# The last unit's output of a recurrent-attention and rational-MLP kernel: two copies on two engines, one transfer per chunk

## The chip, the cores and the metric

The kernel runs on one core of one Trainium2 chip. The metric is the device time of one execution in microseconds (us). A core has five engines with queues of their own: TensorE (PE in the profile; its weight loads are PEld), VectorE (DVE), ScalarE (ACT), GpSimd (POOL) and SyncE (SP, which here only issues transfers). Transfers between HBM and the on-chip memory are issued from the queues of SP, ACT and POOL and moved by 16 DMA engines.

## The reference

Inputs `q`, `k`, `v`, `f_logit` have the shape (4, 8, 768, 48): batch B, heads H, positions S, head size D.

```
f = 1.0 / (1.0 + np.exp(-f_logit))
for t in range(S):
    state = f[:, :, t, :, None] * state + np.einsum('bhd,bhe->bhde', k[:, :, t], v[:, :, t])
    y[:, :, t] = np.einsum('bhd,bhde->bhe', q[:, :, t], state)
x = y.transpose(0, 2, 1, 3).reshape(3072, 384)
h = x @ w_in                                   # 384 -> 2048
P = a[0] + a[1] * h + a[2] * h**2 + a[3] * h**3
Q = 1.0 + abs(b[0]) * abs(h) + abs(b[1]) * h**2
out = (P / (Q + 1e-06)) @ w_out                # 2048 -> 384, float32, (3072, 384)
```

## The kernel before, in words

The 3072 tokens are worked in 12 units, numbered 0 to 11, of 256 tokens each: unit n is block c = n // 4 of positions in batch b = n % 4. A unit has two chunks (j = 0, 1) of C = 128 tokens. The recurrence is done in its chunked form (cumulative sums of log gates on PE, scores, masks, states), and its output x goes through the MLP: `h` (PE, w_in), the rational function on DVE, ACT and by accumulating transfers of POOL, and `o` (PE, w_out).

Nothing is scheduled by a planner. `ORDER` is one written-out list of steps, and each engine's instruction stream is the steps in that order. A step is a name with its arguments: `o 11 1 12 16` is function `o` for unit 11, chunk 1, tiles 12 to 15 of the 16 tiles of 128 that make up 2048. Waits between engines are derived from the tiles that the steps read and write. A wait is on the tile as a whole: what reads a part of tile `op` waits for what was last written to that tile.

The end of the work, which the change concerns, is made of these steps for unit n:

- `gm n m0 m1` (line 444, DVE) finishes tiles m0 to m1 of `gall`, the values P/Q, with the reciprocals `qi` that `ex` (line 412, ACT) made.
- `o n j m0 m1` (line 452, PE) multiplies those tiles by w_out for chunk j and sums into the PSUM tile `op`, whose first index after the partition is the chunk.
- `oe n j0 j1 eng` (in `oe`, line 459) copies chunks j0 to j1 of `op` into the SBUF tile `osb` [128 partitions, 2 chunks, 384 float32]. With `s` ScalarE copies. `osb` has two buffers, so unit 11 takes the buffer that unit 9 used.
- `so n j0 j1 qu` (in `store`, line 467) stores them to HBM.

A chunk's 128 partitions hold its tokens as 2t + i: partition 64 i + t is token 2t + i. `store` therefore issues two transfers from SP: i = 0 for partitions 0 to 63, the even tokens of both chunks, and i = 1 for partitions 64 to 127, the odd tokens of both. Each has 64 partitions x 2 chunks = 128 rows of 384 float32 = 1536 bytes, 192 KB together. The view of the destination is, in (step, count) pairs, (768, 64), (49152, 2), (1, 384).

The last steps of the list, where unit 11's two chunks are accumulated alternately, are

```
o 11 1 8 12; o 11 1 12 16; so 10 0 2 s; o 11 0 12 16; oe 11 0 2 s; so 11 0 2 s
```

Of the kernel before, what the change touches and what calls it, by code (L numbers as in the profile page):

```python
# [28 lines left out]
def kernel(  # L29
# [431 lines left out]
    def store(n, j0, j1, qu="s"):  # L461
        s = unit(n)
        for i in range(2):
            dst = bass.AP(tensor=out.tensor,
                          offset=out.offset + (s["b"] * S + s["c"] * NT + j0 * C + i) * DM,
                          ap=[[2 * DM, R], [C * DM, j1 - j0], [1, DM]])
            (nc.scalar if qu == "a" else nc.sync).dma_start(out=dst, in_=s["osb"][R * i:R * i + R, j0:j1, :])
# [47 lines left out]
```

## Time and profile before

| what | value |
|---|---|
| time, median of 3 runs | 237.08 us (236.73 to 237.97) |
| the profiled execution's own time | 238.7 us |
| its span, first to last instruction | 237.0 us |
| busy in the span | PE 85%, DVE 87%, ACT 85%, POOL 33% |
| ACT copy `osb<-op`, 128x768 | 12 of them, 801 ns on average; the last 0.80 us at 231.46 |
| transfers `out_dram<-osb` | 24, from SP, 192 KB each, median 5.1 us from issue to landing; the last ones 2.7 and 2.8 us |

The span is that of the profiled execution alone; 1.7 us of its own time lie outside it. "Share" of the DMA is the mean busy share of 16 engines. A packet is one row of a transfer, or one small completion write.

### The profile page before, as it was taken

How to read it: one execution, taken by the hardware profiler on the slowest of the kernel's cores; microseconds unless marked ns; L12 is line 12 of the kernel's file. 1: busy time of each engine (PE TensorE's matmuls, PEld its weight loads, DVE VectorE, ACT ScalarE, POOL GpSimd, SP SyncE). 2: the span in 40 equal slices, each digit the busy share in tenths (PEclk: the TensorE clock that was granted, in tenths of full speed). 3: DMA queues.
4: the chain of work that ended last, by engine and by line, in shares of the span. 5: the costliest groups of instructions: out<-in, count | busy, mean ns of one | idle time of the engine just before them, and what ended most of it. 6: DMA issues, size and time to landing. Idle time of an engine off the chain costs nothing.

```text
span 237.0 us, 6907 instructions
## 1 busy us (share of the span) xinstructions
...
## 2 busy tenths in 40 slices
...
GB/s 134 248 223 206 197 204 254 206 215 118 154 260 203 255 240 111 88 117 239 245 255 195 171 232 259 190 251 157 169 198 174 183 88 188 204 170 186 133 142 133
DMA packets 62957, 45.00 MB, mean 190 GB/s; under 512 B 51408, under 2 KB 57296, under 8 KB 62928
## 3 DMA queue, kind: packets, MB, share of 16 engines
...
q14 instruction: 6, 0.05, 0.0%
q10 hardware_dynamic: 144, 0.00, 0.0%
...
## 4 chain that ended last, share of the span: by engine, by line
DVE 28%; ACT 25%; PE 21%; DMA 14%; issue 7%; SPq 3%; ACTq 0%
DMA z<-h 8%; PE hp L345 8%; ACT hy L359 7%; PE op L452 7%; ACT qi L412 6%; DMA kn<-in_k_dram 5%; DVE h L363 5%; DVE gall L431 4%; SPq L110 3%; DVE scm L254 3%; ACT lq L404 3%; DVE gall L444 3%; DVE qkp L212 3%; DVE z L371 3%; PE y L268 2%
## 5 line engine op out<-in xcount | busy, mean ns | idle before, releaser
L452 PE MATMUL op<-w_out_sb,gall 128*128 128x384 bf16 x384 | 71.6, 330 | 2.8 <-DVE gall L444 2.0
L345 PE MATMUL hp<-xT,w_in_sb 128*128 128x256 bf16 x576 | 69.8, 279 | 2.3 <-ACT xT L324 2.2
L345 PEld LDWEIGHTS <-w_in_sb 128*128 128x128 bf16 x576 | 57.1, 100 | 13.2 <-issue 4.0
L359 ACT CAST hy<-hp 128x1024 bf16<-128x1024 f32 x48 | 47.8, 1028 | 7.3 <-PE hp L345 7.1
L452 PEld LDWEIGHTS <-gall 128*128 128x128 bf16 x384 | 35.4, 98 | 27.0 <-DVE gall L444 4.4
L404 ACT ACTIVATE lq<-z 128x2048 f32<-128x2048 bf16 (+1 forms) x25 | 45.5, 1826 | 1.9 <-DMA z<-h 1.8
L412 ACT ACTIVATE qi<-lq 128x2048 bf16<-128x2048 f32 (+1 forms) x26 | 46.4, 1799 | 0.1
L435 POOL DMA_DIRECT2D gall<-hy x21 | 20.2, 992 | 74.2 <-ACT lq L404 18.4
L399 POOL DMA_DIRECT2D z<-h x20 | 18.8, 954 | 49.7 <-DVE z L371 12.6
L363 DVE TENSOR_TENSOR h<-hy 128x2048 bf16<-128x2048 bf16 (+1 forms) x26 | 29.5, 1137 | 4.4 <-ACT hy L359 4.3
L254 DVE TENSOR_TENSOR scm<-sc,mask 128x1024 bf16<-128x1024 f32 x24 | 28.9, 1216 | 2.2 <-PE sc L246 2.2
L444 DVE TENSOR_TENSOR gall<-gall,qi 128x2048 bf16<-128x2048 bf16 (+1 forms) x26 | 29.5, 1139 | 1.0 <-ACT qi L412 1.0
L431 DVE TENSOR_TENSOR gall<-gall,h 128x2048 bf16<-128x2048 bf16 (+1 forms) x26 | 29.2, 1136 | 0.0
L261 POOL COPY vmp<-vn 128x128 bf16<-128x128 bf16 x24 | 25.2, 1126 | 9.7 <-DMA vn<-in_v_dram 9.6
L206 ACT ACTIVATE A<-cs 128x768 f32<-128x768 f32 (+1 forms) x26 | 19.4, 773 | 6.9 <-DVE qkp L212 6.2
L197 PE MATMUL cs<-lsp,Ui 128*128 128x384 bf16 (+1 forms) x39 | 12.1, 373 | 10.5 <-ACT lsp L187 10.1
L224 PE MATMUL tp<-ident,qkp 128*128 128x128 bf16 x192 | 14.6, 234 | 6.2 <-DVE scm L254 3.8
L212 DVE TENSOR_TENSOR qkp<-kn,A 128x768 bf16<-128x768 f32 (+1 forms) x13 | 11.7, 897 | 8.7 <-ACT A L206 4.6
L224 PEld LDWEIGHTS <-qkp 128*128 128x128 bf16 x192 | 12.4, 104 | 8.4 <-DVE qkp L212 6.2
L371 DVE TENSOR_SCALAR z<-hy 128x2048 uint16<-128x2048 uint16 (+1 forms) x26 | 16.7, 652 | 0.0
L182 ACT ACTIVATE fn<-fn 128x768 f32<-128x768 f32 (+1 forms) x13 | 10.6, 813 | 7.0 <-DMA fn<-in_f_logit_dram 7.0
L422 DVE TENSOR_SCALAR hy<-hy,a_sb 128x4096 bf16<-128x4096 bf16 (+1 forms) x13 | 16.4, 1259 | 0.0
...
## 6 DMA issues: line engine op xcount, KB each, us to landing
...
```

Source lines behind the costliest of these rows:

```text
L224: nc.tensor.transpose(t[:, x, i, p, :], s["qk"][:, x, i, 2 * p:2 * p + 2, :].rearrange("t h d -> t (h d)"), ident)
L254: return nc.vector.tensor_mul(t, s["sc", g].rearrange("s r a i t -> s (r a) (i t)"), mb)
L261: nc.gpsimd.tensor_copy(s["vm"][:, :, :, 32 * x:32 * x + 16], src)
L345: nc.tensor.matmul(t[:, m - m0, :].rearrange("f (j t) -> f j t", j=UB), w_in_sb[:, kk, m * P:(m + 1) * P], s["x"][:, :, kk, :], start=(kk ...
L359: nc.scalar.copy(fl(big(s, "hy", "hy", 3), m0, m1), fl(s["hp", m0], 0, m1 - m0))
L363: return nc.vector.tensor_mul(fl(big(s, "h2", "h2", 2), m0, m1), fl(s["hy"], m0, m1), fl(s["hy"], m0, m1))
L371: return nc.vector.tensor_scalar(fl(big(s, "z", "z", 2), m0, m1).bitcast(U16), fl(s["hy"], m0, m1).bitcast(U16), 0x7FFF, None, op0=ALU.bit ...
L404: nc.scalar.activation(fl(lq(s, g), m0 - 8 * g, m1 - 8 * g), fl(s["z"], m0, m1), AF.Ln, scale=regs[2], bias=1.0 + 1e-6)
L412: nc.scalar.activation(fl(s["qi", g], m0 - 8 * g, m1 - 8 * g), fl(s["lq", g], m0 - 8 * g, m1 - 8 * g), AF.Exp, scale=-1.0)
L431: return nc.vector.tensor_mul(fl(s["g"], m0, m1), fl(s["g"], m0, m1), fl(s["h2"], m0, m1))
L444: return nc.vector.tensor_mul(fl(s["g"], m0, m1), fl(s["g"], m0, m1), fl(s["qi", g], m0 - 8 * g, m1 - 8 * g))
L452: nc.tensor.matmul(s["op"][:, j, 0:DM], s["g"][:, m, C * j:C * j + C], w_out_sb[:, m, :], start=(s["on", j] == 1), stop=(s["on", j] == KF))
```

## The change

In the order list, the last four matmul tiles of chunk 0 come before those of chunk 1. Unit 11's copy is then split: chunk 0 by ScalarE, with a store from SP's queue, and chunk 1 by VectorE, with a store from ScalarE's queue. In `store`, a call for one chunk issues one transfer instead of two: its source is all 128 partitions of one chunk, and its destination view is (384, 2), (768, 64), (1, 384), with the parity i as the outermost of its three dimensions.

The other edits of the diff (an argument `hold` on the weight loads, a return value of `ls`, a record of every step's instruction in `marks`) are used by no step of the list and add no instruction.

```diff
-o 11 1 8 12; o 11 1 12 16; so 10 0 2 s; o 11 0 12 16; oe 11 0 2 s; so 11 0 2 s"""
+o 11 1 8 12; so 10 0 2 s; o 11 0 12 16; o 11 1 12 16; oe 11 0 1 s; so 11 0 1 s; oe 11 1 2 v; so 11 1 2 a"""
...
-    def load_w_in(m0, m1):
-        nc.gpsimd.dma_start(out=w_in_sb[:, :, m0 * P:m1 * P],
+    def load_w_in(m0, m1, hold=None):
+        i = nc.gpsimd.dma_start(out=w_in_sb[:, :, m0 * P:m1 * P],
...
+        if hold is not None:
+            behind(i, hold[1:])
...
     def store(n, j0, j1, qu="s"):
         s = unit(n)
+        if j1 - j0 == 1:
+            dst = bass.AP(tensor=out.tensor, offset=out.offset + (s["b"] * S + s["c"] * NT + j0 * C) * DM,
+                          ap=[[DM, 2], [2 * DM, R], [1, DM]])
+            (nc.scalar if qu == "a" else nc.sync).dma_start(out=dst, in_=s["osb"][:, j0, :])
+            return
         for i in range(2):
...
-            mark = args.pop()[1:] if args and args[-1].startswith("!") else None
-            made = steps[name](*(int(x.lstrip("@")) if x.lstrip("@").isdigit() else x for x in args))
-            if mark is not None:
-                marks[mark] = made
+            marks[".".join([name] + [x for x in args if x.isdigit()])] = steps[name](
+                *(int(x.lstrip("@")) if x.lstrip("@").isdigit() else x for x in args))
```

Here DM = 384, R = 64, C = 128.

More of the change, by code (lines that the diff above doesn't have):

```diff
@@ L19 @@
 ORDER = """
-cz 3; cz 0; cu 0; cz 1; ld 0 f 2 4; ci; ld 1 f; cu 1; ab_ b a; ld 0 k 0 2; ld 0 k 2 4; ld 0 v; ld 0 f 0 2; ld 0 q 0 2; ef 0 2 4; ls 0 2 4; fa; ef 0 0 2; ld 0 q 2 4; cz 2; cs 0 2 4 @2; ls 0 0 2; A 0 0 2 4; ld 1 q; cm; ld 2 f; ld 1 k; A 0 1 2 4; vm 0 1; cs 0 0 2 @1; xa 0 1 2 4; ld 1 v; ef 1; ls 1; xa 0 0 2 4; ab_ a s; wi 8 16; A 0 0 0 2; T 0 2 4 @0; vm 0 0; xa 0 0 0 2; A 0 1 0 2; xa 0 1 0 2; wi 4 8; cs 1 @2; Te 0 2 4; ef 2; ld 2 q; wi 0 4; ld 2 k; ld 3 f; T 0 0 2 @0; fr; vm 1 0; A 1 0; Te 0 0 2; sv 0 0 @3; sc 0 0 @1; sc 0 1 @0; A 1 1; ae 0; vm 1 1; st 0 0; ls 2; xa 1 1; cs 2 @2; mk 0 1; sv 0 1; xa 1 0; ld 2 v; wo 4 8; mk 0 0; A 2 1; T 1 @0; A 2 0; yi 0 1 @2; yb 0 2 4; wo 0 4; fb; yb 0 0 2; Te 1 s; st 0 1; sc 1 1 @3; ye 0 s; sc 1 0 @0; h 0 12 16 @1; mk 1 1; xa 2 0; hy 0 12 16; mk 1 0; ld 3 k; h 0 8 12 @2; hy 0 8 12; sq 0 8 16; ab 0 8 16; sv 1 0 @1; ld 3 q; h 0 4 8 @0; ae 1; hy 0 4 8; st 1 0; zv 0 8 16; h 0 0 4 @3; hy 0 0 4; ld 3 v; xa 2 1; yi 1 1 @0; ld 4 f; lz 0 8 16; sv 1 1; yb 1 2 4; yb 1 0 2; T 2 @3; st 1 1; ab 0 0 8; sq 0 0 8; vm 2 0; ye 1 s; Te 2 s; h 1 0 4 @1; p1 0 0 16; ld 4 k; zv 0 0 8; pm 0 0 8; hy 1 0 4; p2 0 0 16; ld 5 f; ef 3; h 1 4 8 @2; pm 0 8 16; hy 1 4 8; h 1 12 16 @1; sc 2 1 @0; ls 3; lz 0 0 8; h 1 8 12 @2; hy 1 8 12; sq 1 0 8; vm 2 1; ta 0 8 16; sv 2 0 @3; ex 0 0 8; ae 2; ab 1 0 8; hy 1 12 16; mk 2 1; ld 4 v; yb 2 2 4 @0; zv 1 0 8; sc 2 0 @2; vm 3 1; ex 0 8 16; st 2 0; yi 2 1; mk 2 0; sq 1 8 16; yb 2 0 2; cs 3 @1; ye 2 s; ab 1 8 16; ld 4 q; A 3 1; ld 5 q; ef 4; A 3 0; zd 1 8 16; p1 1 0 16; gm 0 8 16; h 2 8 12 @2; xa 3 0; pm 1 0 8; ld 6 f; ls 4; h 2 4 8 @0; tv 0 0 8; hy 2 8 12; xa 3 1; p2 1 0 16; h 2 0 4 @1; wo 12 16; wo 8 12; h 2 12 16 @2; hy 2 0 4; hy 2 4 8; T 3 @1; ld 5 k; ld 6 q; sq 2 0 8; ta 1 0 8; gm 0 0 8; hy 2 12 16; lz 1 8 16; cs 4 @2; o 0 0 0 4 @0; o 0 1 4 8; sq 2 8 16; vm 4 0; A 4 0; Te 3 s; ab 2 0 8; zd 2 0 8; sv 2 1; ab 2 8 16; pm 1 8 16; o 0 0 12 16; o 0 1 0 4; vm 3 0; sc 3 0 @1; ld 5 v; st 2 1; ta 1 8 16; ex 1 8 16; ld 7 f; o 0 1 12 16; ld 6 k; mk 3 0; A 4 1; sc 3 1 @3; o 0 0 8 12; mk 3 1; lz 1 0 8; p1 2 0 16; o 0 1 8 12; ex 1 0 8; sv 3 0 @3; yb 3 2 4 @1; xa 4 0; yb 3 0 2; ae 3; ef 5; o 0 0 4 8; oe 0 0 2 s; st 3 0; xa 4 1; yi 3 1; pm 2 8 16; p2 2 0 16; T 4 @2; ye 3 s; h 3 12 16 @0; zv 2 8 16; Te 4 s; h 3 4 8 @1; ta 2 8 16; pm 2 0 8; hy 3 12 16; h 3 0 4 @2; ls 5; so 0 0 2 s; gm 1 0 8; hy 3 4 8; sv 3 1; ta 2 0 8; ld 7 k; ld 7 q; sc 4 0 @0; hy 3 0 4; st 3 1; mk 4 0; ab 3 0 8; sv 4 0 @1; gm 1 8 16; sq 3 0 8; vm 5 0; lz 2 0 8; h 3 8 12 @2; o 1 1 0 4 @3; zd 3 0 8; o 1 1 4 8; ld 8 f; hy 3 8 12; o 1 1 12 16; ex 2 0 8; o 1 0 0 4; p1 3 0 16; cs 5 @2; lz 2 8 16; A 5 1; sq 3 8 16; o 1 0 8 12; vm 5 1; sc 4 1 @0; mk 4 1; ae 4; ab 3 8 16; ex 2 8 16; o 1 0 4 8; ld 6 v; vm 4 1; st 4 0; o 1 1 8 12; yb 4 0 2 @0; yb 4 2 4; yi 4 1; ef 6; zv 3 8 16; pm 3 0 8; yi 4 0; ye 4 s; pm 3 8 16; gm 2 8 16; h 4 8 12 @0; A 5 0; lz 3 8 16; p2 3 0 16; hy 4 8 12; h 4 12 16 @2; ta 3 0 8; xa 5 0; o 1 0 12 16; hy 4 12 16; h 4 4 8 @0; xa 5 1; ef 7; h 4 0 4 @2; sq 4 8 16; sv 4 1; tv 3 8 16; hy 4 4 8; oe 1 0 2 s; hy 4 0 4; T 5 @0; ab 4 8 16; ab 4 0 8; zd 4 8 16; o 2 0 8 12 @3; o 2 1 8 12; ld 7 v; Te 5 s; gm 2 0 8; lz 3 0 8; sq 4 0 8; zd 4 0 8; sc 5 1 @2; st 4 1; ex 3 8 16; sv 5 0 @0; o 2 1 4 8; o 2 0 12 16; mk 5 1; ls 6; vm 6 0; sc 5 0 @1; o 2 1 12 16; o 2 1 0 4; ex 3 0 8; p1 4 0 16; vm 6 1; ld 9 f; yb 5 2 4 @2; ae 5; ld 9 q; mk 5 0; gm 3 8 16; yi 5 0; st 5 0; lz 4 8 16; so 1 0 2 s; yb 5 0 2; o 2 0 0 4; p2 4 0 16; cs 6 @1; yi 5 1; ye 5 s; pm 4 8 16; pm 4 0 8; o 2 0 4 8; A 6 1; h 5 8 12 @2; A 6 0; ls 7; oe 2 0 2 s; xa 6 1; ta 4 8 16; hy 5 8 12; xa 6 0; vm 7 0; h 5 0 4 @1; ld 8 k; hy 5 0 4; gm 3 0 8; sv 5 1; T 6 @3; st 5 1; Te 6; so 2 0 2 s; h 5 12 16 @2; ex 4 8 16; hy 5 12 16; ef 8; tv 4 0 8; ld 8 v; ab 5 8 16; h 5 4 8 @0; sv 6 0 @3; sq 5 8 16; ae 6; hy 5 4 8; ld 8 q; o 3 1 0 4 @1; o 3 0 8 12; zd 5 8 16; lz 4 0 8; sq 5 0 8; cs 7 @2; o 3 0 0 4; sc 6 0 @0; ab 5 0 8; ld 10 f; A 7 1; ld 9 k; mk 6 0; zd 5 0 8; st 6 0; o 3 1 8 12; ls 8; sc 6 1 @0; A 7 0; ex 4 0 8; yi 6 1 @2; yb 6 0 2; sv 6 1; yi 6 0; p1 5 0 16; o 3 0 12 16; mk 6 1; yb 6 2 4; gm 4 8 16; pm 5 8 16; p2 5 0 16; o 3 1 4 8; ye 6 s; lz 5 8 16; h 6 0 4 @0; ta 5 8 16; o 3 1 12 16; vm 8 0; pm 5 0 8; o 3 0 4 8; st 6 1; ef 9; h 6 4 8 @2; xa 7 0; oe 3 0 2 s; hy 6 0 4; ta 5 0 8; hy 6 4 8; h 6 8 12 @3; gm 4 0 8; vm 7 1; xa 7 1; h 6 12 16 @0; hy 6 8 12; sq 6 0 8; T 7 @3; ld 10 q; ld 11 f; hy 6 12 16; ab 6 0 8; cs 8 @0; vm 8 1; zd 6 0 8; o 4 0 0 4 @2; sq 6 8 16; ld 10 k; Te 7 s; sv 7 0 @3; sc 7 0 @1; ab 6 8 16; A 8 1; lz 5 0 8; o 4 1 0 4; zd 6 8 16; o 4 0 12 16; so 3 0 2 s; ae 7; p1 6 0 16; ex 5 8 16; mk 7 0; o 4 1 8 12; yi 7 0 @1; pm 6 8 16; o 4 1 12 16; o 4 1 4 8; A 8 0; yb 7 0 2; ex 5 0 8; o 4 0 8 12; p2 6 0 16; pm 6 0 8; ta 6 8 16; ta 6 0 8; lz 6 0 8; xa 8 1; st 7 0; o 4 0 4 8; sc 7 1 @0; oe 4 0 2 s; yi 7 1; mk 7 1; sv 7 1; xa 8 0; yb 7 2 4; T 8 @0; ye 7 s; lz 6 8 16; gm 5 0 8; h 7 8 12 @1; ld 11 k; Te 8; ld 9 v; h 7 12 16 @2; hy 7 8 12; sc 8 0 @0; st 7 1; gm 5 8 16; sc 8 1 @1; mk 8 0; h 7 0 4 @3; ls 9; hy 7 12 16; ef 10; mk 8 1; sv 8 0 @2; ex 6 8 16; ab 7 8 16; sq 7 8 16; h 7 4 8 @1; so 4 0 2 s; yi 8 0 @0; ae 8; yb 8 2 4; zd 7 8 16; hy 7 0 4; yb 8 0 2; st 8 0; yi 8 1; gm 6 8 16; hy 7 4 8; sq 7 0 8; cs 9 @2; o 5 0 0 4 @1; ye 8 s; A 9 1; ab 7 0 8; ex 6 0 8; vm 9 1; zd 7 0 8; ld 10 v; ef 11; A 9 0; h 8 4 8 @3; o 5 0 8 12; o 5 1 8 12; h 8 0 4 @0; p1 7 0 16; hy 8 4 8; xa 9 1; o 5 1 4 8; hy 8 0 4; h 8 12 16 @3; p2 7 0 16; pm 7 8 16; pm 7 0 8; o 5 0 12 16; h 8 8 12 @0; o 5 1 0 4; xa 9 0; ta 7 8 16; T 9 @2; ta 7 0 8; lz 7 8 16; hy 8 12 16; o 5 1 12 16; ab 8 0 8; sq 8 0 8; gm 6 0 8; hy 8 8 12; ld 11 q; ab 8 8 16; sq 8 8 16; o 5 0 4 8; ls 10; p1 8 0 16; vm 10 1; Te 9 s; zd 8 0 8; oe 5 0 2 s; sv 9 0 @3; o 6 1 8 12 @2; ae 9; zd 8 8 16; st 9 0; so 5 0 2 s; ex 7 8 16; sc 9 0 @1; lz 7 0 8; sc 9 1 @0; o 6 0 4 8; vm 9 0; o 6 0 8 12; o 6 1 0 4; ex 7 0 8; mk 9 1; mk 9 0; o 6 0 0 4; pm 8 8 16; o 6 0 12 16; yi 9 0 @3; yi 9 1; yb 9 2 4; p2 8 0 16; yb 9 0 2; cs 10 @1; o 6 1 12 16; ld 11 v; ta 8 8 16; pm 8 0 8; ye 9 s; A 10 0; A 10 1; h 9 0 4 @0; ta 8 0 8; xa 10 0; xa 10 1; h 9 4 8 @1; hy 9 0 4; gm 7 8 16; T 10 @0; hy 9 4 8; gm 7 0 8; h 9 8 12 @3; sq 9 0 8; lz 8 0 8; Te 10; h 9 12 16 @1; hy 9 8 12; o 6 1 4 8; hy 9 12 16; ab 9 0 8; oe 6 0 2 s; zd 9 0 8; o 7 0 0 4 @3; o 7 1 12 16; sq 9 8 16; ex 8 0 8; o 7 1 0 4; o 7 0 8 12; ab 9 8 16; sc 10 1 @0; ls 11; p1 9 0 16; vm 10 0; sc 10 0 @1; mk 10 0; zd 9 8 16; o 7 0 12 16; o 7 0 4 8; sv 10 0 @2; lz 8 8 16; o 7 1 8 12; ae 10; mk 10 1; ex 8 8 16; st 10 0; pm 9 8 16; yi 10 0 @1; yb 10 0 2; p2 9 0 16; yi 10 1; vm 11 1; yb 10 2 4; ye 10 s; cs 11 @0; o 7 1 4 8; pm 9 0 8; vm 11 0; ta 9 0 8; A 11 1; xa 11 1; A 11 0; oe 7 0 2 s; ta 9 8 16; h 10 4 8 @1; xa 11 0; h 10 0 4 @0; hy 10 4 8; hy 10 0 4; so 7 0 2 s; gm 8 8 16; h 10 8 12 @3; ab 10 0 8; sq 10 0 8; so 6 0 2 s; zd 10 0 8; T 11 @2; hy 10 8 12; h 10 12 16 @0; Te 11; lz 9 8 16; hy 10 12 16; lz 9 0 8; gm 8 0 8; sv 11 0 @1; o 8 1 12 16 @2; sc 11 1 @3; yi 11 0 @0; ab 10 8 16; o 8 0 0 4; o 8 0 8 12; mk 11 1; ae 11; ex 9 0 8; sq 10 8 16; o 8 1 8 12; st 11 0; sc 11 0 @3; o 8 0 4 8; zd 10 8 16; yb 11 2 4; mk 11 0; yi 11 1; ex 9 8 16; p1 10 0 16; o 8 0 12 16; pm 10 8 16; yb 11 0 2; o 8 1 4 8; ye 11 s; o 8 1 0 4; p2 10 0 16; lz 10 0 8; h 11 0 4 @3; ta 10 8 16; pm 10 0 8; gm 9 0 8; hy 11 0 4; h 11 8 12 @1; gm 9 8 16; ta 10 0 8; hy 11 8 12; lz 10 8 16; sq 11 0 4; h 11 4 8 @0; h 11 12 16 @3; o 9 0 12 16 @1; hy 11 4 8; hy 11 12 16; ab 11 0 4; ab 11 8 12; sq 11 8 12; sq 11 4 8; o 9 1 8 12; zd 11 8 12; o 9 0 4 8; ab 11 4 8; zd 11 0 4; o 9 0 0 4; sq 11 12 16; ex 10 8 16; o 9 1 4 8; o 9 0 8 12; p1 11 0 8; ab 11 12 16; ex 10 0 8; zd 11 12 16; u 11 4 8 @0; ln 11 4 8; pm 11 4 8; o 9 1 12 16; gm 10 8 16; o 9 1 0 4; p2 11 0 8; ta 11 4 8; lz 11 8 12; pm 11 0 4; ta 11 0 4; o 10 0 12 16 @3; o 10 1 12 16; gm 10 0 8; p1 11 8 16; o 10 0 8 12; lz 11 0 4; o 10 1 8 12; ex 11 4 8; p2 11 8 16; pm 11 12 16; pm 11 8 12; oe 8 0 2 s; o 10 0 0 4; o 10 1 0 4; gm 11 4 8; so 8 0 2 s; o 10 1 4 8; oe 9 0 2 s; o 10 0 4 8; o 11 0 4 8 @2; tv 11 8 12; ex 11 0 4; gm 11 0 4; o 11 1 4 8; o 11 1 0 4; o 11 0 0 4; ex 11 8 12; lz 11 12 16; gm 11 8 12; o 11 0 8 12; tv 11 12 16; ex 11 12 16; oe 10 0 2 s; so 9 0 2 s; gm 11 12 16; o 11 1 8 12; o 11 1 12 16; so 10 0 2 s; o 11 0 12 16; oe 11 0 2 s; so 11 0 2 s"""
```

9 lines of the change are left out of this document (6 added, 3 removed).

## The prediction

> **What bounds the kernel now.** The change touches the last few us only, so I read what follows the last matmul, not the shares of the page. First the chain of work that ended last, cut to 231 us on (columns: start, length, what):
>
> ```profile
> 230.94 0.50 PE op L452 x3
> 231.44 0.02 issue
> 231.46 0.80 ACT osb L459
> ```
>
> PE ends at 231.44, ACT copies both chunks for 0.80 us, to 232.26, and no instruction that the chain counts follows. The rest, to 237.0, is transfers and the closing of the program. SP's queue, in a window around the copy's end and in one up to the end of the span:
>
> ```profile
> 232.29 0.59 SPq L467 DMA_DIRECT2D out_dram<-osb  x1
> ...
> 232.29 1.25 SPq L467 DMA_DIRECT2D out_dram<-osb  x2
> ```
>
> The two last stores are issued at 232.29 and 0.6 us later. Busy time by stretches (engines, then clock, DMA share, GB/s):
>
> ```profile
> 232.90:233.50 0.60, 0.00 (x0) 0.00 (x0) 0.00 (x0) 0.00 (x0) 0.00 (x0) 1.00 0.00 0
> 233.50:234.50 1.00, 0.00 (x0) 0.00 (x0) 0.00 (x0) 0.00 (x0) 0.00 (x0) 1.00 0.90 186
> 234.50:235.30 0.80, 0.00 (x0) 0.00 (x0) 0.00 (x0) 0.00 (x0) 0.00 (x0) 0.52 0.83 259
> 235.30:237.00 1.70, 0.00 (x0) 0.00 (x0) 0.00 (x0) 0.00 (x0) 0.00 (x0) 0.50 0.00 0
> ```
>
> The DMA engines are quiet until 233.5, so 1.2 us pass from issue to first packet. The two stores move from 233.5 to 235.3 on nearly all 16 engines (shares 0.90 and 0.83). Then 1.7 us remain for the last landing and the closing. No engine computes, so nothing hides a longer transfer. Packets of three windows, 233 to 237, 233.5 to 234.4 and 234.6 to 234.9, each with the share of its queue:
>
> ```profile
> DMA packets 288, 0.39 MB, mean 98 GB/s; under 512 B 32, under 2 KB 288, under 8 KB 288
> q1 hardware_dynamic: 288, 0.39, 39.2%
> ...
> DMA packets 109, 0.17 MB, mean 186 GB/s; under 512 B 0, under 2 KB 109, under 8 KB 109
> q1 hardware_dynamic: 109, 0.17, 89.9%
> ...
> DMA packets 82, 0.12 MB, mean 384 GB/s; under 512 B 7, under 2 KB 82, under 8 KB 82
> q1 hardware_dynamic: 82, 0.12, 105.7%
> ```
>
> The first pair is the whole of the two stores: 2 x 128 rows of 1536 bytes and 32 small writes, which is 16 completions for each. So each store ran on all 16 engines, 8 rows on each. The second pair gives the time of a row while one store moves alone: 0.899 x 16 engines x 0.9 us / 109 = 119 ns. The third, with both in flight: 1.057 x 16 x 0.3 us / 75 rows = 68 ns with the 7 small writes taken as free, 62 ns over all 82 packets; the small ones can't cost nothing, so I use 67.
>
> **The change part by part.**
>
> *Matmul order.* Chunk 0's last four matmuls now come before chunk 1's. Both sets need the same last `gall` piece, and the waits in the built program put the copy of chunk 0 behind the last matmul of the unit, because `op` is one tile: the same count on PE as before. No gain, no loss: the copy starts at 231.46 still.
>
> *ScalarE's copy, now 128x384.* The exponential from PSUM (line 206) takes 826 ns at 768 columns and 477 at 384; the copy takes 801 at 768. Taking off the same 349 gives 0.45 us, so it ends at 231.91 and SP issues chunk 0's store at 231.94 instead of 232.29, 0.35 us earlier. SP is free then: the stores of unit 10 were issued at 229.88 for 1.25 us. Their packets end by 232.9 (the share after it is 0.00), so the new store meets none of them.
>
> *VectorE's copy, 128x384, new.* "Side by side" does not hold: in the built program it waits for ScalarE's copy, as both write the one tile `osb`. Its other waits are stores of units up to 9, long landed. Nothing is queued behind it on VectorE. The trace has no such copy; the nearest row from PSUM is the state product (line 336), 128x384 from float32, 551 ns, an upper end; from below 0.35 us, half of the 688 ns of the 128x1024 bf16 copy (line 232). I take 0.55, the same size and source: it ends at 232.48.
>
> *Chunk 1's store from ScalarE's queue.* It waits for VectorE's copy; only the end of the program is behind it. Its issue is at about 232.51, and with SP's 1.2 us its first packet comes at 233.71. SP issues one transfer less (0.6 us), but that one would come after chunk 0's store and is worth nothing of its own.
>
> *The form of the stores.* This decides. Chunk 0's first packet comes at 231.94 + 1.2 = 233.15. Each store still has 128 rows, but its destination view leads with a dimension of 2. Every store and load of the kernel before has 64 or 128 as the leading count on both sides, and the stores counted above used 16 engines. If a transfer is dealt to the engines in equal blocks of its leading dimension, a lead of 2 leaves two blocks: two engines, 64 rows each, while 14 stand idle. The trace has no transfer with a short lead, so I bound it. From below: still 16 engines, 8 rows each. From above: one engine, all 256 rows. I take two, as source and destination must be cut alike and the destination has only two blocks, and I take the same two engines for both stores, as both have the same form. That is 128 rows each, one after another: 128 x 67 ns = 8.6 us. I take 67 ns rather than 119 because the 119 was seen when 16 engines read one half of the partitions together; two engines that read a half each crowd less than either row. Keeping 119 as an upper end gives 15.2 us.
>
> The Trainium skill states the rule behind this on its page "DMA: Bandwidth & Descriptors", in the section "Why a DMA increments its semaphore by 16 and not by 1": the number of engines is the largest up to 16 that divides the slowest dimension of both views, and on these two queues it is the lowest-numbered ones. No run here shows it yet; by it, 128 and 2 give two engines, the same for both stores. Its specifications give some 27 GiB/s for an engine, by which the 196,608 bytes of each would take 6.8 us (an estimate from that page) and the time would be 241.7 us.
>
> *Sum.* First packet 233.15 + 8.6 = 241.75 for the last row, against 235.3: +6.4 us. The last 1.7 us stay. The span becomes 243.4, and the profiled execution 238.7 + 6.4 = 245.1. That execution was 1.6 us above the median of the runs; 6.4 us at the tail carry over whole: 237.08 + 6.4 = 243.5 us.
>
> **The rivals.**
>
> *All 16 engines are used whatever the lead.* For it: the source still leads with 128 partitions. Against it: the destination can't be cut in 16 equal blocks at its lead. Then chunk 1's rows end at 233.71 + 8 x 67 ns = 234.25, 1.05 us earlier than 235.3; at 119 ns for all 16 rows of an engine 233.15 + 1.9 = 235.05, 0.25 earlier. Between: 236.4 us (236.0 to 236.8). It decides the sign: with 8 engines, 32 rows each, the last row would end at 233.15 + 2.14 = 235.29, as now.
>
> *Two engines for each store, but not the same ones,* the ScalarE queue having others. Then chunk 1 ends last: 233.71 + 64 x 67 ns = 238.0, +2.7 us, 239.8 us. Nothing in the profile speaks for it; that the two queues differ is all.
>
> *Slower still.* Rows at 119 ns on the two engines: 233.15 + 15.2 = 248.4, +13.1, 250.1 us; one engine for everything: 256 x 67 ns = 17.2, +15.0, 252.1 us. Against it: two engines leave the memories nearly idle.
>
> **How the numbers follow.** Two shared engines 0.76; two each, not shared, 0.06; slower still 0.05; all 16 engines 0.11, of which 0.09 within 0.5% and 0.02 faster (only if it saves over 1.2 us); 0.02 for a gain by something that I don't see. About 0.5%, or 1.2 us, is what a measurement of this kernel can tell from no change. So: faster 0.04, same 0.09, slower 0.87. The predicted time is that of two shared engines. The range: down to the unshared case, 239.8, taken as 239.5; up to rows of 85 ns on the two engines, a third of the way from 67 to 119 (128 x 85 ns = 10.9 us, +8.75, 245.8), taken as 246. It leaves out the 16 engines, the gain and the slower cases, 0.18.
>
> **What will show it.** In the profile after: 4 completion writes instead of 32 after 233 us, and a DMA share near 2/16 = 0.12 for some 8 us; VectorE's copy behind ScalarE's, not beside it; SP's last issue near 231.94; everything up to 231.4 as before. The forecast is wrong if the share after 233 us is again 0.8 or more. It is mis-sized if the share is 0.12 for 4.5 or for 15 us.

## The result, and the profile after

The changed kernel takes 244.87 us (median of 4 runs, 243.7 to 246.13) against 237.12 us before (236.73 to 237.97): a ratio of 1.034, with a 95% interval from 1.028 to 1.040. It is 7.75 us slower; 6.4 were forecast, and 244.87 lies in the range. Some executions take a per cent or more longer whatever the kernel: the times and ratios of the experiments leave them out, while the profiles of the kernel before and of the lead of 8, read for their tails, are of such executions.

The profiled execution has a span of 242.0 us. Its end, as the chain of waits has it (start, length, what):

```profile
228.06 1.49 PE op L456 x8
229.55 0.02 issue
229.57 0.49 ACT osb L463
230.06 0.02 issue
230.09 0.56 DVE osb L463
```

The last matmul ends at 229.55 here, where it was 231.44 before; the two executions differ by that much before the changed steps begin (the last `gm` starts at 227.31 here and at 229.20 before), so I compare from the last matmul on. From its end to the end of the span (the tail, in what follows) it is 242.0 - 229.55 = 12.45 us, against 237.0 - 231.44 = 5.56 before: 6.9 us more. The copies and the issues, in order of time:

```profile
229.57 0.48 ACT L463 COPY osb<-op 128x384 f32<-128x384 f32 x1 [1.61 <-PE op L456]
230.08 0.61 SPq L470 DMA_DIRECT2D out_dram<-osb  x1
230.09 0.56 DVE L463 COPY osb<-op 128x384 f32<-128x384 f32 x1 [2.08 <-ACT osb L463]
230.67 1.12 ACTq L470 DMA_DIRECT2D out_dram<-osb  x1
```

VectorE's copy starts when ScalarE's has ended, so they are not side by side. Both transfers are issued by 230.67. The rest is transfer, in stretches (engines, clock, DMA share, GB/s):

```profile
231.30:235.00 3.70, 0.00 (x0) 0.00 (x0) 0.00 (x0) 0.00 (x0) 0.00 (x0) 0.62 0.13 37
235.00:240.30 5.30, 0.00 (x0) 0.00 (x0) 0.00 (x0) 0.00 (x0) 0.00 (x0) 0.50 0.13 48
240.30:242.00 1.70, 0.00 (x0) 0.00 (x0) 0.00 (x0) 0.00 (x0) 0.00 (x0) 0.50 0.00 0
```

A share of 0.13 of 16 engines is two engines busy without a pause, for 9.0 us; before, the same bytes took 1.8 us at 0.83 to 0.90. The last 1.7 us are as they were. The packets from 231.2 to the end:

```profile
DMA packets 260, 0.39 MB, mean 36 GB/s; under 512 B 4, under 2 KB 260, under 8 KB 260
```

The same 256 rows, and 4 completion writes instead of 32: two for each store.

### The profile page after: what moved, and what is told of

Its sections match the earlier page's. It is cut to its first block, busy times and chain, and to the rows that moved or that the text cites. A ratio compares the mean times of both kernels' runs of the same rounds, so it can differ in the third digit from the quotient of the medians.

```text
span 242.0 us, 6911 instructions
## 1 busy us (share of the span) xinstructions
PE 199.6 (82%) x3035; PEld 142.4 (59%) x3036; DVE 207.9 (86%) x246; ACT 200.5 (83%) x196; POOL 80.5 (33%) x96
## 4 chain that ended last, share of the span: by engine, by line
DVE 27%; ACT 25%; DMA 16%; PE 16%; issue 7%; SPq 3%; ACTq 0%
DMA z<-h 12%; ACT hy L363 8%; ACT qi L416 6%; PE hp L349 6%; PE op L456 5%; DMA kn<-in_k_dram 5%; DVE h L367 4%; DVE gall L435 4%; SPq L110 3%; DVE scm L258 3%; ACT lq L408 3%; DVE gall L448 3%; DVE qkp L216 3%; ACT qkT L236 2%; DVE z L375 2%
## 5 line engine op out<-in xcount | busy, mean ns | idle before, releaser
L456 PE MATMUL op<-w_out_sb,gall 128*128 128x384 bf16 x384 | 70.4, 327 | 2.9 <-DVE gall L448 2.1
L403 POOL DMA_DIRECT2D z<-h x20 | 20.6, 1047 | 49.7 <-issue 12.0
L265 POOL COPY vmp<-vn 128x128 bf16<-128x128 bf16 x24 | 27.5, 1258 | 11.3 <-DMA vn<-in_v_dram 11.3
L421 DVE TENSOR_SCALAR gall<-hy,a_sb 128x4096 bf16<-128x4096 bf16 (+1 forms) x13 | 16.3, 1257 | 0.0
```

Of the source, the lines that this page charges most:

```text
L265: nc.gpsimd.tensor_copy(s["vm"][:, :, :, 32 * x:32 * x + 16], src)
L456: nc.tensor.matmul(s["op"][:, j, 0:DM], s["g"][:, m, C * j:C * j + C], w_out_sb[:, m, :], start=(s["on", j] == 1), stop=(s["on", j] == KF))
```

## The experiments

On the later occasions whole runs of one kernel lay several us apart (the kernel before: 236.92 to 239.96 on the second), so a difference of the tail is read from the tail, in the profile, and the ratio is given beside it where there is one.

### Each store as transfers that lead with 64

```diff
         if j1 - j0 == 1:
-            dst = bass.AP(..., ap=[[DM, 2], [2 * DM, R], [1, DM]])
-            (nc.scalar if qu == "a" else nc.sync).dma_start(out=dst, in_=s["osb"][:, j0, :])
+            for i in range(2):
+                dst = bass.AP(... + i) * DM, ap=[[2 * DM, R], [1, DM]])
+                (nc.scalar if qu == "a" else nc.sync).dma_start(out=dst, in_=s["osb"][R * i:R * i + R, j0, :])
```

> The changed kernel with each chunk's store issued as two transfers that lead with 64 (even tokens, odd tokens), two from SP's queue and two from ScalarE's; copies and order as in the change. The tail is the time from the last matmul's end to the end of the span: 5.56 us before, 12.45 us after. Theory 'engines' (a lead of 2 leaves two engines, shared by both stores): 16 engines again, tail 5.0 to 5.4 us, time 236.3 to 237.0 us. Rival 'queue' (ScalarE's queue starts its transfer late, 4.35 us from issue to first packet in the profile after): the late start stays, tail 8 us or more, 239.5 us or more. Rival 'copies' (the second copy behind the first, on VectorE, costs the time): as slow as the change, 244 us.

The last matmul ends at 229.93 and the span at 235.2: a tail of 5.3 us, against 5.56 before and 12.45 after. Two runs took 235.6 and 237.0 us, beside 236.9 to 240.0 of before; that is too few for a ratio. The packets from 231.1 on, with the queues of ScalarE (q10) and SP (q1):

```profile
DMA packets 356, 0.42 MB, mean 103 GB/s; under 512 B 80, under 2 KB 356, under 8 KB 356
q1 hardware_dynamic: 196, 0.23, 20.7%
q10 hardware_dynamic: 160, 0.20, 19.8%
```

Both queues are in use and the copies are as serial as in the change, yet the whole loss is gone. ScalarE's queue moves 128 rows and 32 completion writes, 16 for each of its two transfers. (SP's rows here include the end of unit 10's store.) This excludes the copies and the second queue as the cause. As forecast by the engines theory.

### The new form alone

```diff
-... oe 11 0 1 s; so 11 0 1 s; oe 11 1 2 v; so 11 1 2 a
+... oe 11 0 2 s; so 11 0 1 s; so 11 1 2 s
```

> The kernel before (matmul order, one copy of both chunks by ScalarE) with only the stores in the new form: one transfer per chunk whose destination leads with 2, both from SP's queue. Engines: first packet 2.0 us after the last matmul, 128 rows of 65 ns and some 0.7 us of stalls as in the profile after, 1.7 us to the end: tail 12.7 us, time 244.2 us (243.3 to 245.5). Queue: ScalarE's queue is not used, so tail under 6 us, 237 us. Copies: as before, 237 us.

Median 242.98 us, a little under the 243.3 to 245.5 expected; the ratio to before is 1.022, a wide interval from 1.005 to 1.039. The tail is 241.1 - 228.48 = 12.6 us, as expected. From 230.4 to the end, and the stretches:

```profile
DMA packets 260, 0.39 MB, mean 36 GB/s; under 512 B 4, under 2 KB 260, under 8 KB 260
...
230.50:239.50 9.00, 0.00 (x0) 0.00 (x0) 0.00 (x0) 0.00 (x0) 0.00 (x0) 0.54 0.13 44
```

With one copy, one queue and nothing else of the change, the form of the store costs the tail what the change costs it: two engines for 9.0 us, 4 completions.

### Leads of 4 and 8

Unit 11's tokens are dealt to the partitions in L blocks, by copying its xT in pieces in mid-kernel (not shown here); the store then leads with L, written for 4 and for 8 alike below.

```diff
-                          ap=[[DM, 2], [2 * DM, R], [1, DM]])
+                          ap=[[DM, L], [L * DM, C // L], [1, DM]])
```

> The changed kernel with unit 11's tokens dealt to partitions in four blocks instead of two (the scaled copy into xT is made in 4 pieces on ScalarE, which may cost up to 0.5 us in mid-kernel), so that the destination leads with 4. Engines: four engines, 32 rows each of each store; first packet 1.74 us after the last matmul, 64 rows of 65 ns = 4.2 us and 0.3 us of stalls, 1.7 us: tail 7.9 us, time 239.5 us (238.8 to 240.5), 8 completion writes. A fixed penalty for any short lead: tail 12.4 us as with 2, 244 us. Queue: over 8 us of tail from the late start.

> The same with eight blocks (xT copy in 8 pieces, up to 1.0 us in mid-kernel), so that the destination leads with 8. Engines: eight engines, 16 rows each of each store; first packet 1.74 us after the last matmul, ScalarE's store at 2.3 us, 32 rows of 65 ns = 2.1 us: last row at 3.9 us, tail 5.6 us, time 236.8 to 238.5 us, 16 completion writes. A fixed penalty for any short lead: tail 12.4 us, 244 us. Queue: over 8 us of tail.

With 4 the median is 243.18 us, the ratio 1.019 (1.008 to 1.030) and the tail 241.1 - 232.52 = 8.6 us; with 8 they are 237.83 us, 0.999 (0.994 to 1.004) and 238.8 - 232.62 = 6.2 us. The packets and the stretch of the rows, first for 4:

```profile
DMA packets 264, 0.39 MB, mean 57 GB/s; under 512 B 8, under 2 KB 264, under 8 KB 264
...
234.30:239.40 5.10, 0.00 (x0) 0.00 (x0) 0.00 (x0) 0.00 (x0) 0.00 (x0) 0.62 0.25 77
```

and for 8:

```profile
DMA packets 272, 0.39 MB, mean 87 GB/s; under 512 B 16, under 2 KB 272, under 8 KB 272
...
234.40:237.10 2.70, 0.00 (x0) 0.00 (x0) 0.00 (x0) 0.00 (x0) 0.00 (x0) 1.00 0.48 146
```

Shares of 0.25 and 0.48 are 4 and 8 engines of 16, and 8 and 16 completions are 4 and 8 for each store: as many engines as blocks, and no fixed penalty. Both tails came out 0.6 to 0.7 us over the forecast. The time with 8 lies in its range; that with 4 is 2.7 us over the 238.8 to 240.5 expected, of which the tail explains 0.7. On this occasion the kernel before took 238.5 us and not 237.1, which is 1.4 us more; no run shows where the rest comes from. The rows took 9.0, 5.1 and 2.7 us for 128, 64 and 32 rows on an engine; at 65 ns a row that is 8.3, 4.2 and 2.1, so such stores take some 0.6 to 0.9 us more, of which I had allowed 0.3 as stalls with 4 and none with 8. SP's store, which comes first, has the slow rows: while alone, until 237.0 with 4 and until 235.8 with 8, its rows took 96 and 103 ns (0.240 x 16 x 2.8 us / 112 and 0.442 x 16 x 1.5 us / 103).

### A long lead that 16 doesn't divide

The run with leads of 64 again, its loop over the partitions cut in two:

```diff
+                for r0, r1 in ((0, 62), (62, 64)):
+                    (...).dma_start(out=dst[r0:r1], in_=s["osb"][R * i + r0:R * i + r1, j0, :])
```

> The chunk stores of the run with a lead of 64, each cut into a transfer of 62 partitions and one of 2. If any long lead is spread over 16 engines and only short leads are confined: the four small transfers, 2 rows on 2 engines, cost their issues only (up to 1.2 us on each queue), tail 5.5 to 7 us. If the number of engines has to divide the lead (62 is 2 x 31): two engines for every transfer, 128 rows each as in the change, tail 12 to 13.5 us, and some 16 completion writes instead of 136 or so.

The tail is 246.0 - 233.49 = 12.5 us. From 235.3 on, and the stretch of the rows:

```profile
DMA packets 264, 0.38 MB, mean 36 GB/s; under 512 B 16, under 2 KB 264, under 8 KB 264
...
235.20:244.60 9.40, 0.00 (x0) 0.00 (x0) 0.00 (x0) 0.00 (x0) 0.00 (x0) 0.53 0.13 41
```

62 partitions, on both sides of the transfer, run on two engines, with 2 completions for each of 8 transfers. So shortness isn't the point: the count of engines has to divide the lead. Whether it is the largest number up to 16 that divides it, or the largest power of two, these leads (2, 4, 8, 62, 64, 128) don't tell, since both give the same here. This was one run (247.88 us), read for its tail alone.

### One transfer per chunk that leads with 128

Unit 11's xT is written in natural order of the tokens, so that the partition is the token.

```diff
+        if n == 11:
+            for j in range(UB):
+                i = nc.scalar.mul(t[:, j].rearrange("p k (t i) -> p k i t", i=2),
+                                  s["y"][:, j, 0:KD * C].rearrange("p (k i t) -> p k i t", k=KD, i=2), regs[0])
+            return i
...
-                          ap=[[DM, 2], [2 * DM, R], [1, DM]])
+                          ap=[[DM, C], [1, DM]])
```

> The changed kernel with unit 11's tokens in their natural order on the partitions (its scaled copy into xT is made in two pieces that write every other column, up to 0.2 us in mid-kernel), so that each chunk is one transfer whose destination leads with 128. Engines: 16 engines, 8 rows each per store; SP's first packet 1.75 us after the last matmul, ScalarE's at 2.3, last row at 2.9 to 3.3, tail 4.6 to 5.0 us against 5.56, time 0.998 of before (0.995 to 1.002). Queue, if ScalarE's late start is its own: tail over 8 us. Copies: tail over 6 us.

The tail is 236.1 - 231.73 = 4.4 us, 1.2 less than before and a little under the forecast: SP's first row came some 1.4 us after the last matmul, at about 233.1, and not 1.75. The ratio, 0.997 (0.992 to 1.002), doesn't separate it from before. The copies and issues:

```profile
231.75 0.48 ACT L468 COPY osb<-op 128x384 f32<-128x384 f32 x1 [1.60 <-PE op L461]
232.26 0.37 SPq L475 DMA_DIRECT2D out_dram<-osb  x1
232.27 0.56 DVE L468 COPY osb<-op 128x384 f32<-128x384 f32 x1 [2.08 <-ACT osb L468]
232.86 0.35 ACTq L475 DMA_DIRECT2D out_dram<-osb  x1
```

These are the change's steps at the change's times; only the lead is another. Issues take 0.35 us where they took 0.6 before, and from 233.7 to 234.4

```profile
q10 hardware_dynamic: 143, 0.20, 77.4%
```

gives 0.774 x 16 x 0.7 us = 8.7 us for ScalarE's 128 rows: 68 ns each, with the 15 small writes taken as free. SP's store, alone from 233.3 to 233.6, has 0.978 x 16 x 0.3 us / 68 rows = 69 ns. The half-partition stores needed 119 before and 115 in the run with leads of 64 (1.002 x 16 x 0.3 us / 42 rows, from 232.3 to 232.6), each while one moved alone.

### A tile for each chunk, in SBUF and in PSUM

```diff
+        if n == 11:
+            s["osb", j0] = ms.tile([P, 1, DM], F32, name=f"osl{j0}", bufs=1)
```

> The same with a tile of its own for each chunk of unit 11's output, so that VectorE's copy needn't wait for ScalarE's. Engines, with the copies side by side as the change had it in mind: both copies start with the last matmul's end, issues at 0.54 and 0.62 us, first packets at 1.75 and 1.8, 16 rows on each of 16 engines in 1.07 to 1.9 us: last row at 2.85 to 3.65, tail 4.5 to 5.3 us; time 0.997 of before (0.993 to 1.001). If the serial copies were worth more than a few tenths, tail under 4.4 us.

The tail is 232.6 - 228.25 = 4.4 us. VectorE's copy still started 0.51 us after ScalarE's, at 228.78 after 228.27, and ScalarE's copy is what ended its wait:

```profile
228.78 0.56 DVE L468 COPY osl<-op 128x384 f32<-128x384 f32 x1 [2.08 <-ACT osl L468]
```

Both read the one PSUM tile, which I take for the reason; no run shows that by itself. So this expectation failed in its condition, and the serial copies weren't tested by it. The ratio, 0.988 (0.981 to 0.995), is lower than the 0.997 that the same tail gave the run before, so part of it may not be the tail's. Two more runs asked whether that part lasts, one of the same kernel and one of the kernel before with only an additional tile for unit 11:

> The kernel of the run token_sep, unchanged, on another occasion. Its tail (4.42 us) was that of token_lead128 while its time stood 0.9 of a per cent lower, so something other than the tail differed. If that was chance in the body of the kernel: ratio to before 0.995, from the tail's 1.16 us, within 0.990 to 1.000. If it is lasting: 0.988 (0.982 to 0.992) again.

> The kernel before, with only a tile of its own for unit 11's output, two chunks wide, copied by ScalarE and stored as before. The tail can't change (5.56 us) since the copy waits for the last matmul. If the extra tile, which moves where tiles lie, makes the body faster: ratio about 0.993. If not: 1.000, within 0.996 to 1.004.

They gave 0.994 (0.990 to 0.998) and 0.997 (0.992 to 1.001), the latter with its tail at 234.7 - 229.16 = 5.5 us. The tail's 1.2 us are 0.5% and explain the 0.994; the additional tile by itself shows no effect beyond its interval. The rest of the 0.988 I take for chance, which these runs fit but don't prove. Then, with a PSUM tile of its own for each chunk:

```diff
-o 11 1 4 8;
+o 11 1 4 8 @0;
...
+            if n == 11:
+                s["op", j] = s["op"]
```

> The same with a PSUM tile of its own for each chunk too, so that chunk 0 is copied and stored while chunk 1's last four matmuls run. Chunk 0's copy ends before the last matmul; chunk 1's starts with its end, 0.56 us, issue at 0.62, first packet at 1.8, 8 rows of 67 to 119 ns: last row at 2.35 to 2.75, tail 4.05 to 4.45 us, 1.1 to 1.5 us less than before; time 0.995 of before (0.990 to 0.999).

The tail is 234.2 - 229.68 = 4.5 us, over the 4.05 to 4.45 expected, and the ratio 1.002 (0.996 to 1.008). Here chunk 0 was copied while chunk 1's last matmuls ran, as meant:

```profile
229.06 0.48 ACT L470 COPY osl<-op 128x384 f32<-128x384 f32 x1 [0.95 <-PE op L463]
229.56 0.46 SPq L480 DMA_DIRECT2D out_dram<-osl  x1
229.71 0.56 DVE L470 COPY osl<-op 128x384 f32<-128x384 f32 x1 [1.57 <-PE op L463]
230.30 0.35 ACTq L480 DMA_DIRECT2D out_dram<-osl  x1
```

Chunk 0's copy begins 0.62 us before the last matmul's end at 229.68, and VectorE's 0.03 us after it. ScalarE's issue comes 0.62 us after that end instead of 1.13. Yet nothing is won, because the DMA engines are full before and while they come:

```profile
229.70:230.70 1.00, 0.00 (x0) 0.00 (x0) 0.56 (x1) 0.00 (x0) 0.00 (x0) 1.00 0.96 238
230.70:231.50 0.80, 0.00 (x0) 0.00 (x0) 0.00 (x0) 0.00 (x0) 0.00 (x0) 1.00 0.98 246
231.50:232.50 1.00, 0.00 (x0) 0.00 (x0) 0.00 (x0) 0.00 (x0) 0.00 (x0) 0.60 0.77 284
```

Unit 10's stores, issued shortly before, still move: from 229.3, where their rows begin, to 231.1 SP's queue moved 249 rows, and they alone have 256. The rows of unit 11 come behind them. An earlier copy meets DMA engines that aren't free.

## Why the prediction was right

*The form of the stores* decided, as forecast: two engines, the same for both stores, 128 rows one after another. The form alone reproduces the tail (12.6 us), undoing it alone removes it (5.3), and leads of 4 and 8 give 4 and 8 engines. The Trainium skill's rule, on its page "DMA: Bandwidth & Descriptors" in the section "Why a DMA increments its semaphore by 16 and not by 1" (the engines used are the largest number up to 16 that divides both views' slowest dimension), agrees with all of these runs, and with the 62 partitions on two engines, which a rule about short leads alone would have put on more.

*The sum.* Against the tail's 6.9 us the forecast had 6.4. First row: 1.71 us after the last matmul forecast, 1.75 seen (231.30 - 229.55). Rows: 8.6 us forecast, 9.0 seen, so 70 ns a row on the average where 67 was taken. They were not even. From 231.2 to 233.1 and from 237.6 to 240.3 the queues that moved show

```profile
q1 hardware_dynamic: 34, 0.05, 12.6%
...
q10 hardware_dynamic: 88, 0.13, 13.0%
```

which is 0.126 x 16 x 1.9 us / 34 = 113 ns for the first rows, and 0.130 x 16 x 2.7 us / 86 = 65 ns for the later ones (2 of the 88 are completions). So the 67 ns fit the later rows, and the reason given for choosing it over 119 failed: the prediction put the 119 ns down to 16 engines reading one half of the partitions together, but two engines alone had rows of 113 ns at first. That this lasted 2 us and not the whole 9 was luck for the sum; why it is so, no run shows. Closing: 1.7 us, as forecast. The medians differ by 7.75 us, 0.9 more than the tails; the interval of the ratio, 1.028 to 1.040, is 6.7 to 9.4 us, so the tail's 6.9 may be the whole of it.

*The copies.* ScalarE's took 0.48 us (0.45 forecast), VectorE's 0.56 (0.55), one behind the other. The copy didn't start earlier for the new order of matmuls. All as forecast; but the reason given for the wait, that both copies write the one tile `osb`, isn't enough, as VectorE's still waited when each chunk had an SBUF tile of its own.

*ScalarE's store* was wrong in one step: its first packet was to come 1.2 us after its issue, as it did on SP's queue. It came at about 235.0, some 4.35 us after it. Until 235.0 every row was of SP's queue (q1), then both move, in equal numbers:

```profile
DMA packets 89, 0.14 MB, mean 36 GB/s; under 512 B 0, under 2 KB 89, under 8 KB 89
q1 hardware_dynamic: 89, 0.14, 12.8%
...
DMA packets 83, 0.12 MB, mean 48 GB/s; under 512 B 2, under 2 KB 83, under 8 KB 83
q10 hardware_dynamic: 42, 0.06, 7.2%
q1 hardware_dynamic: 41, 0.06, 6.1%
```

These are the windows from 231.2 to 235.0 and from 235.0 to 237.6. It cost nothing that the runs show: the two engines had rows all the time, the sum only counts rows, and with both stores in SP's queue the rows took the same 9.0 us.

*The rivals.* All 16 engines would have shown 32 completions and a share near 0.9; two unshared engines a share of 0.25 while both queues move, where 7.2% and 6.1% are 0.13 together. Neither was there. Rows of 119 ns throughout would have taken 15.2 us; only the first 2 us had rows near that.
